# A hand-ordered attention and feed-forward kernel: a new order of the same words, whole score steps from the start, the residual sum written into its own input tile

## The chip, the cores and the metric

The kernel runs on one core of one Trainium2 chip. The core has a matrix engine (PE, whose weight loads the profile lists apart as PEld), a vector engine (DVE), an activation engine (ACT), a general engine (POOL) and a queue processor that here only issues DMAs (SP). Each engine works through its own instructions in order; semaphores tie the engines together. The metric is the device time of one launch in microseconds (us); lower is better.

## The reference, cut to what matters

Attention with a hash mask, then layer norm and a two-layer feed-forward with a residual sum. Batch 4, 8 heads, 768 positions, head size 64, model width 512, hidden width 2048.

```python
q_bits = (np.einsum('bhsd,dk->bhsk', q, proj) > 0)        # 6 bits for each query; the same for keys
mask   = q_bucket[:, :, :, None] == k_bucket[:, :, None, :]
scores = np.where(mask, scale * q @ k.T, -1e9)
attn   = softmax(scores)
x      = (attn @ v) brought to [batch, seq, 512]
xn     = (x - mean) / sqrt(var + 1e-6) * g_ln
out    = x + relu(xn @ w_ch1) @ w_ch2
```

## The kernel before

The work is cut into 12 units `u`, three for each batch; a unit has 256 queries of all 8 heads. The heads are two groups `g` of four. A unit and a group have three score steps, each for 256 keys (`kp`), so step `s` runs from 0 to 71 with `u = s // 6`, `g = (s % 6) // 3`, `kp = s % 3`. The mask is not applied as such: for each query and key the six bits, held as +0.5 and -0.5 in the tile `G`, are multiplied with each other by PE and added to the score before the exponential, so that only an equal bucket gives a weight that is not negligible. A row in which no key has the query's bucket must give the mean of the values, so the sum of the values over all 768 positions (`vsB`) is added with a factor of 2 to the power of -100.

Nothing in the program decides the order. The text `ORDER` lists some 1,100 words, `name.engine.numbers`, and a loop at the end calls a function for each word, in that order (engine: `t` PE, `v` DVE, `a` ACT, `p` POOL, `s` SP). Each engine thus gets its instructions in the order of its words; waits come from the tiles that the words read and write, and from their buffers. The words that matter here:

- `lx`, `LX`: load queries or keys (128 to 768 KB) of batch 0 or of a later batch into an `X` tile (4 buffers). `lv`: values (768 KB for batch 0, 192 KB each for later ones) into `vnat` (2 buffers). `lw1`, `lw2`: a quarter of a weight matrix, issued by POOL, since it is cast to bf16 on the way. `lg`: the norm's gain.
- Batch 0: `tn` (DVE) transposes a third of a tile, `ca` casts it (queries, t = 0, with a factor; keys, t = 1), `ha` (PE, fp32, 4 matmuls, line 312) projects onto the hash vectors with the matrix `pfull` that `pf` builds, `bi` (DVE) makes bits. Later batches: `tu` (DVE, eight a head group) transposes into a `T` tile (2 buffers), `CA` casts it, `hm` (PE, line 403) projects, `bt` (DVE) makes bits, and 16 `mo` copies (DMAs of 4.5 KB) bring them to `G`.
- `cv` (POOL) casts values into `vaug`; `on` writes its column of ones. `su` (POOL, lines 369 to 371) adds the values up over 6 blocks; `sp` (PE, line 376) sums over the 128 partitions with a matrix of ones; `sc` copies the result to `vsB`.
- `S.t.s.h` (PE, line 438): the scores of a step, 24 matmuls in sets of four that lie on four strips of 32 rows, into two tiles of two PSUM banks each, `scA` for heads 0 and 1, `scB` for 2 and 3. With h = 2 the word does all four heads, with 0 or 1 only two of them. `E.a.s.h` (ACT, line 444): the exponential of one tile. `A.t.s.h` (PE, line 453): 16 matmuls of the weights with `vaug`, into the tile `acc` (two banks), summed over three steps.
- `na`, `nb`, `nc` (DVE): normalize `acc` into `x(u)` and take statistics. `ce` (DVE, lines 482 and 483): mean, variance, and the centred tile `xc`. `rs` (POOL): 1 / sqrt(var). `fl` (SP): transposes `xc` by DMA into `xnT`; for unit 0 `ft` (PE) and `fc` do this instead.
- `F.t.u.p` (PE, line 510): 8 matmuls, two of the 16 blocks of the hidden layer, into one bank `f1` (unit 0: `f1` and `f2` in turn). `R` (DVE line 520 or ACT line 518): relu into `hb`. `D.t.u.t.q` (PE, line 526): a quarter of the second layer, 4 matmuls of 512 columns into the bank `f2`; the last half tile of unit 11 in 256 columns, with `scA` and `scB`. `Z` (DVE, line 534): the result times 1 / sqrt(var), plus `x`. `O` (line 544): stores 32 partitions of the result.

PSUM is full: scA 2, scB 2, acc 2, f1 1, f2 1 banks. So the next S must wait for E, the next F for R, the next D for Z, the next group's A for na.

In `ORDER` of before, the steps 2, 1 and 0, with which the kernel begins, are done as halves (`S.t.2.0`, `S.t.2.1` and so on); all later ones whole. SP issues nearly all DMAs: ACT issues the load of `proj` and six of the last stores.

Of the kernel before, what the change touches and what calls it, by code (L numbers as in the profile page):

```python
# [8 lines left out]
F32 = mybir.dt.float32  # L9
# [29 lines left out]
F.t.1.1 R.v.1.1 A.t.12.2 A.t.13.2 F.t.1.0 R.v.1.0 S.t.15.2 E.a.15.1 mo.s.1.0.2.1 LX.s.2.0.1 F.t.1.5 R.v.1.5
mo.s.1.0.3.0 lw2.p.3 D.t.0.0.3 mo.s.1.0.3.1 E.a.15.0 mo.s.1.0.1.2 hm.t.1.1 S.t.17.2 E.a.17.0 E.a.17.1 mo.s.1.0.1.3  # L40
su.p.1.4 mo.s.1.0.2.0 na.v.2.0 A.t.16.2 nb.v.2.0 A.t.15.2 nc.v.2.0 bt.v.1.1 mo.s.1.1.1.0 mo.s.1.1.0.0 mo.s.1.1.0.3
mo.s.1.1.2.0 mo.s.1.1.3.1 F.t.1.7 mo.s.1.1.3.2 Z.v.0.0 D.t.0.1.0 S.t.18.2 E.a.18.0 E.a.18.1 CA.v.1.1.0 tu.v.2.0.1.3
tu.v.2.0.1.0 R.v.1.7 A.t.17.2 mo.s.1.1.1.3 mo.s.1.1.1.1 F.t.1.4 R.a.1.4 mo.s.1.1.1.2 D.t.0.1.1 D.t.0.1.2 sp.t.1.0
sc.a.1.0 mo.s.1.1.0.1 na.v.2.1 nb.v.2.1 nc.v.2.1 ce.v.2.0 fl.s.2.0 ce.v.2.1 D.t.0.1.3 mo.s.1.1.0.2 F.t.1.3 R.v.1.3
S.t.20.2 E.a.20.0 E.a.20.1 F.t.1.6 Z.v.0.1 D.t.1.0.0 D.t.1.0.1 D.t.1.0.2 rs.p.2 R.a.1.6 D.t.1.0.3 CA.p.1.1.1
tu.v.2.0.0.2 sp.t.1.4 fl.s.2.1 mo.s.1.1.2.2 tu.v.2.0.1.1 mo.s.1.1.3.3 S.t.19.2 E.a.19.1 mo.s.1.1.2.3 mo.s.1.1.3.0
mo.s.1.1.2.1 tu.v.2.0.0.1 O.s.0.1 sc.v.1.4 F.t.2.7 O.s.0.2 cv.p.1.0.2 lv.s.2.0.0 lv.s.2.0.1 A.t.18.2 A.t.20.2
cv.p.1.4.2 lv.s.3.0.1 rs.p.1 Z.v.1.0 LX.s.2.1.0 R.v.2.7 F.t.2.4 R.v.2.4 E.a.19.0 S.t.21.2 E.a.21.0 D.t.1.1.0
E.a.21.1 O.s.0.0 F.t.2.0 A.t.19.2 lv.s.2.0.3 tu.v.2.0.1.2 na.v.3.0 nb.v.3.0 tu.v.2.0.0.3 R.a.2.0 lv.s.2.0.2 S.t.22.2
E.a.22.0 E.a.22.1 F.t.2.1 R.a.2.1 su.p.2.0 LX.s.2.1.1 A.t.21.2 D.t.1.1.1 LX.s.3.0.0 tu.v.2.0.0.0 S.t.23.2 E.a.23.1  # L50
# [12 lines left out]
ce.v.4.1 fl.s.4.1 rs.p.4 D.t.3.0.1 S.t.35.2 E.a.35.0 E.a.35.1 hm.t.2.1 bt.v.2.1 mo.s.2.1.2.1 tu.v.3.0.0.2
mo.s.2.1.0.2 tu.v.3.0.1.1 tu.v.3.0.0.1 mo.s.2.1.0.3 mo.s.2.1.2.2 mo.s.2.1.1.0 D.t.3.0.2 F.t.3.6 R.a.3.6 O.s.2.2
mo.s.2.0.2.2 mo.s.2.1.3.1 lv.s.2.4.0 cv.p.2.4.0 mo.s.2.1.0.1 mo.s.2.1.3.2 mo.s.2.1.2.3 S.t.34.2 E.a.34.1 E.a.34.0
# [52 lines left out]
def kernel(  # L118
# [15 lines left out]
    nc = tc.nc  # L134
# [78 lines left out]
    def xt(u):  # L213
        return sb(f"x{u}", [P, 2, DM], F32, "x", 3)
# [374 lines left out]
```

## Time and profile before

| what | us |
|---|---|
| median of 3 runs | 313.65 |
| lowest and highest run | 312.13, 322.8 |
| span of the profiled execution | 311.1 |

The span runs from the first to the last instruction of the profiled execution; the time of a run also has what lies around it, about 2.5 us. The busy time of PE contains waiting inside a run of matmuls, since a matmul's end is modelled. More of the profile's rows:

| group (line, engine) | instructions | mean ns | busy us |
|---|---|---|---|
| f, first layer (510, PE) | 768 | 273 | 99.3 |
| sc, scores (438, PE) | 1728 | 267 to 273 | 96.0 |
| acc, weights times values (453, PE) | 1152 | 194 | 44.6 |
| exponential (444, ACT) | 144 | 1110 | 152.7 |
| relu (520, DVE) | 52 | 690 | 35.9 |
| relu (518, ACT) | 44 | 597 | 26.1 |
| transpose of a later batch (243, DVE) | 48 | 553 | 24.9 |
| query cast of a later batch (252, POOL) | 3 | 4243 | 12.7 |
| sums of values (369, 370, 371, POOL) | 24 | 1819, 853, 809 | 27.9 |
| copy to G (415, issued by SP) | 96 | 721 | |

Eight instructions of 273 ns that start 109 ns apart take 0.87 us, not 8 x 273: on PE the distance of starts counts. The profile's chain of waits goes back from the last instruction to what released it, step by step; "issue" in it is time in which an engine waited for nothing that the profile shows. DMAs moved 33.58 MB, most of it in the first 54 us. The granted clock of PE was 0.998 over the span.

### The profile page before, as it was taken

How to read it: one execution, taken by the hardware profiler on the slowest of the kernel's cores; microseconds unless marked ns; L12 is line 12 of the kernel's file. 1: busy time of each engine (PE TensorE's matmuls, PEld its weight loads, DVE VectorE, ACT ScalarE, POOL GpSimd, SP SyncE). 2: the span in 40 equal slices, each digit the busy share in tenths (PEclk: the TensorE clock that was granted, in tenths of full speed). 3: DMA queues.
4: the chain of work that ended last, by engine and by line, in shares of the span. 5: the costliest groups of instructions: out<-in, count | busy, mean ns of one | idle time of the engine just before them, and what ended most of it. 6: DMA issues, size and time to landing. Idle time of an engine off the chain costs nothing.

```text
span 311.1 us, 9787 instructions
## 1 busy us (share of the span) xinstructions
PE 294.3 (95%) x4296; PEld 206.5 (66%) x4336; DVE 185.7 (60%) x357; ACT 181.5 (58%) x197; POOL 89.7 (29%) x103
## 2 busy tenths in 40 slices
PE   7997799799999899989999999999999999999995
PEld 6675587576677557667667666667667676775663
DVE  3578868768442984978364668443544547246432
ACT  2666687454678655665456787655666777661000
POOL 0869570602403650416705304300300101001000
PEclk9999999999999999999999999999999999999999
DMA  7999999840299317511430901401300400502122
GB/s 177 286 301 361 238 208 261 91 125 9 42 244 300 128 24 179 166 38 35 100 79 2 204 8 30 87 11 33 94 2 2 103 0 13 93 2 60 43 70 68
DMA packets 30426, 33.58 MB, mean 108 GB/s; under 512 B 15536, under 2 KB 27056, under 8 KB 30384
## 3 DMA queue, kind: packets, MB, share of 16 engines
q1 hardware_dynamic: 25792, 28.50, 36.0%
q0 software_dynamic: 4224, 4.19, 8.3%
q8 instruction: 34, 0.56, 0.7%
q10 hardware_dynamic: 368, 0.26, 0.3%
q14 instruction: 8, 0.07, 0.1%
HBM read 27.53 MB, written 6.29 MB: 109 GB/s over the span
## 4 chain that ended last, share of the span: by engine, by line
PE 73%; DMA 14%; POOL 4%; DVE 4%; issue 3%; SPq 1%; DVEq 0%; POOLq 0%
PE f L510 25%; PE sc L438 13%; PE acc L453 8%; DMA vn<-in_v_dram 8%; DMA w_sb<-in_moe_w_ch_dram 5%; POOL t L369 2%; PE hp L403 1%; POOL vaug L361 1%; DMA xnT<-xc 1%; PE f_100None L526 1%; PE f L526 1%; PE f_81None L526 1%; PE f_50None L526 1%; PE f_60None L526 1%; PE f_90None L526 1%
## 5 line engine op out<-in xcount | busy, mean ns | idle before, releaser
L444 ACT ACTIVATE E<-sc,bias_sb 128x1024 bf16<-128x1024 f32 x144 | 152.7, 1110 | 72.3 <-PE sc L438 71.3
L510 PE MATMUL f<-xnT,w_sb 128*128 128x256 bf16 x768 | 99.3, 273 | 1.5 <-DVE B L246 1.2
L510 PEld LDWEIGHTS <-w_sb 128*128 128x128 bf16 x768 | 70.9, 98 | 23.6 <-issue 10.0
L520 DVE TENSOR_SCALAR hb<-f 128x512 bf16<-128x512 f32 x52 | 35.9, 690 | 58.9 <-PE f L510 58.3
L526 PEld LDWEIGHTS <-hb 128*128 128x128 bf16 x400 | 37.5, 98 | 36.0 <-issue 5.1
L438 PE MATMUL sc<-qb,kb 32*128 32x256 bf16 x1152 | 53.4, 267 | 0.0
L518 ACT ACTIVATE hb<-f 128x512 bf16<-128x512 f32 x44 | 26.1, 597 | 39.5 <-PE f L510 39.5
L453 PEld LDWEIGHTS <-E 128*128 128x128 bf16 x1152 | 41.1, 98 | 6.5 <-issue 4.3
L438 PE MATMUL sc<-G 6*128 6x256 bf16 x576 | 42.6, 273 | 2.4 <-DVE G L246 1.3
L453 PE MATMUL acc<-vaug,E 128*128 128x65 bf16 x1152 | 44.6, 194 | 0.0
L488 POOL TENSOR_SCALAR rs<-mv 128x2 f32<-128x2 f32 x12 | 7.1, 594 | 99.8 <-DVE mv L482 99.5
L438 PEld LDWEIGHTS <-kb 32*128 32x128 bf16 x1152 | 31.1, 93 | 1.6
L438 PEld LDWEIGHTS <-G 6*128 6x128 bf16 x576 | 15.6, 91 | 22.2 <-issue 18.2
L243 DVE STREAM_TRANSPOSE T<-X 128x384 f32<-128x384 f32 x48 | 24.9, 553 | 0.8 <-POOL kb L254 0.8
L369 POOL TENSOR_TENSOR t<-vn 128x768 f32<-128x768 f32 x8 | 14.6, 1819 | 33.4 <-DMA vn<-in_v_dram 33.3
L466 DVE SCALAR_TENSOR_TENSOR y<-vsB,acc 128x520 f32<-128x520 f32 x24 | 16.6, 691 | 10.9 <-PE acc L453 10.8
L483 DVE SCALAR_TENSOR_TENSOR xc<-x,mv,gB 128x512 bf16<-128x512 f32 x24 | 22.5, 938 | 0.8
L252 POOL TENSOR_SCALAR qb<-T 128x1536 bf16<-128x1536 f32 x3 | 12.7, 4243 | 28.4 <-DVE mv L482 15.5
L361 POOL CAST vaug<-vn 128x768 bf16<-128x768 f32 x16 | 13.5, 854 | 20.1 <-DMA vn<-in_v_dram 20.1
L475 DVE TENSOR_TENSOR x<-y,rc 128x512 f32<-128x512 f32 x24 | 18.7, 778 | 0.8
L479 DVE BATCH_NORM_STATS2 st<-x 128x6 f32<-128x256 f32 x48 | 18.0, 417 | 0.7
L312 PE MATMUL hf<-tp,pfull 128*128 128x256 f32 x48 | 14.9, 450 | 0.7 <-DVE pfull L277 0.7
(96 smaller groups left out, 229.6 us busy)
## 6 DMA issues: line engine op xcount, KB each, us to landing
out_dram<-res SPq DMA_DIRECT2D x44, 128.0 KB
X<-in_k_dram SPq DMA_DIRECT2D x7, 768.0 KB
vn<-in_v_dram SPq DMA_DIRECT2D x24, 192.0 KB
X<-in_q_dram SPq DMA_DIRECT2D x6, 768.0 KB
w_sb<-in_moe_w_ch_dram POOLq DMA_DIRECT2D x8, 512.0 KB, 12.5
vn<-in_v_dram SPq DMA_DIRECT2D x2, 768.0 KB
G<-B SPq DMA_DIRECT2D x96, 4.5 KB
X<-in_q_dram SPq DMA_DIRECT2D x2, 512.0 KB
```

Of the source, the lines that this page charges most:

```text
L243: nc.vector.transpose(d[:, j], s[:, j, kj0 : kj0 + n])
L369: nc.gpsimd.tensor_tensor(t3, s[:, 0:3], s[:, 3:6], op=AOP.add)
L438: nc.tensor.matmul(sc(s, i // 2)[:, i % 2, 256 * kk : 256 * kk + 256], lh, rh, start=(rep == 0), stop=(rep == 2), skip_group_check=True,)
L444: nc.scalar.activation(E(s)[:, heads(h)], sc(s, h), AF.Exp, scale=EXP_SCALE, bias=bias_sb)
L453: nc.tensor.matmul(acc[:, qt, (D + 1) * i : (D + 1) * (i + 1)], E(s)[:, i, 256 * kk + P * qt : 256 * kk + P * qt + P], vaug(u // 3)[:, 4 * ...
L475: nc.vector.tensor_tensor(xo, a[:, :, :, 0:D], rc.to_broadcast([P, 2, 4, D]), op=AOP.mult)
L479: nc.vector.bn_stats(stats(u)[:, qt, g], xt(u)[:, qt, 256 * g : 256 * g + 256])
L483: nc.vector.scalar_tensor_tensor(xc(u)[:, t], xt(u)[:, t], mv(u)[:, t, 0:1], gB, op0=AOP.subtract, op1=AOP.mult,)
L510: nc.tensor.matmul(f1[:, n].rearrange("p (t x) -> p t x", t=2), w1_sb[:, dt, P * nt : P * nt + P], xnT(u)[:, :, dt], start=(dt == 0), stop ...
L518: nc.scalar.activation(hb(u)[:, 2 * p : 2 * p + 2], f1, AF.Relu)
L520: eng.tensor_scalar_max(hb(u)[:, 2 * p : 2 * p + 2], f1, 0.0)
L526: nc.tensor.matmul(f2, hb(u)[:, nt, P * t : P * t + P], w2_sb[:, nt, half(h)], start=(nt == 0), stop=(nt == NNT - 1),)
```

## The change

Four edits and a new `ORDER`.

- A score tile's banks: for the steps 2, 1, 0 (`ROT`) the six half-step tiles go in turn over scA, scB and acc. In `ORDER` these three steps are now whole words (`S.t.2.2`, `A.t.2.2`).
- `Z` writes its result into `x(u)`, `O` stores from there, and the tile `res` (2 buffers) is gone. `x` and `E` have 4 buffers in place of 3. So a buffer of `x` comes free when its stores have landed.
- For batch 0 the two `su` and `sp` words are replaced by `sq`: six matmuls of ones with `vaug` itself, summed in PSUM.
- The order is new everywhere, and so are some engines: 27 `mo`, 7 `lv`, 3 `LX`, one `lx` and 27 `O` words (6 before) are issued by ACT; the query casts of later batches on POOL are one (`CA.p.2.0.0`) in place of three; `R` stands 55 times on DVE (52 before); all `sc` are on DVE.

```diff
+ROT = (2, 1, 0)
...
     def xt(u):
-        return sb(f"x{u}", [P, 2, DM], F32, "x", 3)
+        return sb(f"x{u}", [P, 2, DM], F32, "x", 4)
...
-    def res(u):
-        return sb(f"res{u}", [P, 2, DM], F32, "res", 2)
...
     def E(s):
-        return sb(f"E{s}", [P, 4, 512], BF16, "E", 3)
+        return sb(f"E{s}", [P, 4, 512], BF16, "E", 4)
...
+    def sq(eng, b, hs):
+        p = ps(f"vp{b}{hs}", [P, 512], "f1")[:, :256].rearrange("p (h d) -> p h d", d=D)
+        for kj in range(KJ):
+            nc.tensor.matmul(p, ones, vaug(b)[:, hs : hs + 4, kj, 0:D], start=(kj == 0), stop=(kj == KJ - 1))
...
     def sc(s, h):
-        return ps(f"sc{s}{h}", [P, 2, 512], ("scA", "scB")[h])
+        tag = ("scA", "scB", "acc")[(2 * ROT.index(s) + h) % 3] if s in ROT else ("scA", "scB")[h]
+        return ps(f"sc{s}{h}", [P, 2, 512], tag)
...
     def Z_(eng, u, t, h=None):
         nc.vector.scalar_tensor_tensor(
-            res(u)[:, t, half(h)], made[f"f2_{u}{t}{h}"], rstd(u)[:, t : t + 1], xt(u)[:, t, half(h)],
+            xt(u)[:, t, half(h)], made[f"f2_{u}{t}{h}"], rstd(u)[:, t : t + 1], xt(u)[:, t, half(h)],
...
-            out=out_view[u // 3][u % 3][c][:, t, half(h)], in_=res(u)[32 * c : 32 * c + 32, t, half(h)],
+            out=out_view[u // 3][u % 3][c][:, t, half(h)], in_=xt(u)[32 * c : 32 * c + 32, t, half(h)],
```

The new order from its beginning to the first F words:

```text
mem.v pmem.p warm.t lx.s.0.0.0.1 lx.s.0.1.1.3 lp.a pf.v tn.v.0.0.0 ha.t.0.0.0 tn.v.0.1.2 lx.s.1.0.0.1 tab.a
bi.v.0.0.0 ca.a.0.0.0 tn.v.0.1.1 lx.s.0.1.0.1 ha.t.0.1.2 bi.v.0.1.2 ha.t.0.1.1 ca.a.0.1.2 S.t.2.2 tn.v.0.1.0
lx.a.0.0.1.3 tn.v.1.0.0 E.a.2.0 bi.v.0.1.1 lx.s.1.1.0.3 ha.t.1.0.0 ca.v.1.0.0 bi.v.1.0.0 ca.p.0.1.1 p32.p lv.s.0.0.4
ca.p.0.1.0 S.t.1.2 tn.v.1.1.0 ha.t.0.1.0 bi.v.0.1.0 tn.v.1.1.1 ca.p.1.1.0 E.a.2.1 ca.p.1.1.1 E.a.1.0 S.t.0.2
cv.p.0.0.0 on.p.0 lv.s.0.4.4 cv.p.0.0.2 ha.t.1.1.1 bi.v.1.1.1 tn.v.1.1.2 lg.s ca.p.1.1.2 cv.p.0.4.0 ha.t.1.1.0
bi.v.1.1.0 E.a.1.1 E.a.0.0 cv.p.0.4.2 lx.s.1.0.1.3 E.a.0.1 LX.s.1.0.1 S.t.4.2 E.a.4.0 lw1.p.3 tn.v.0.0.1 E.a.4.1
ha.t.1.1.2 A.t.2.2 lv.s.1.4.2 A.t.1.2 S.t.3.2 lv.s.1.4.0 bi.v.1.1.2 tn.v.1.0.2 lv.s.1.4.3 sq.t.0.0 E.a.3.0
tu.v.1.0.1.0 LX.s.1.1.0 ca.p.0.0.1 lw1.p.2 A.t.0.2 sc.v.0.0 E.a.3.1 lv.s.1.0.2 tn.v.1.0.1 ca.a.1.0.1 ha.t.0.0.1
tu.v.1.0.1.2 na.v.0.0 S.t.5.2 E.a.5.0 E.a.5.1 lv.s.1.0.0 A.t.3.2 bi.v.0.0.1 sq.t.0.4 sc.v.0.4 S.t.8.2 E.a.8.0
nb.v.0.0 nc.v.0.0 E.a.8.1 tu.v.1.0.1.1 lw1.p.1 A.t.4.2 lv.s.1.4.1 A.t.5.2 ha.t.1.0.1 tn.v.0.0.2 ca.a.0.0.2 bi.v.1.0.1
S.t.6.2 cv.p.1.4.0 E.a.6.0 na.v.0.1 E.a.6.1 ha.t.1.0.2 lw1.p.0 lw2.p.1 nb.v.0.1 nc.v.0.1 bi.v.1.0.2 ha.t.0.0.2
S.t.7.2 A.t.8.2 ce.v.0.1 lw2.p.0 LX.s.1.0.0 bi.v.0.0.2 E.a.7.0 ce.v.0.0 ft.t.0.1 fc.v.0.1 A.t.6.2 ft.t.0.0
tu.v.1.0.0.2 ca.v.1.0.2 E.a.7.1 fc.a.0.0 tu.v.1.0.0.1 LX.a.1.1.1 S.t.9.2 lw2.p.2 tu.v.1.0.0.3 E.a.9.1 A.t.7.2
tu.v.1.0.1.3 E.a.9.0 F.t.0.6 rs.p.0 R.v.0.6 na.v.1.0 F.t.0.7 R.a.0.7 su.p.1.4 S.t.10.2 sp.t.1.4 sc.v.1.4 F.t.0.5
...
```

Two stretches further on, and the end:

```text
...
tu.v.1.1.1.3 mo.s.1.0.1.0 mo.a.1.0.3.0 R.v.1.0 na.v.2.0 F.t.1.2 R.a.1.2 S.t.15.2 E.a.15.1 nb.v.2.0 Z.v.0.0
tu.v.1.1.1.0 mo.s.1.0.0.3 hm.t.1.1 bt.v.1.1 mo.s.1.1.3.1 su.p.1.0 mo.s.1.1.1.1 D.t.0.1.0 F.t.1.1 mo.s.1.1.0.2
...
na.v.3.1 E.a.24.1 hm.t.2.0 bt.v.2.0 CA.p.2.0.0 mo.s.2.0.0.1 LX.a.2.1.1 mo.s.2.0.2.2 S.t.26.2 F.t.2.3 E.a.26.0
nb.v.3.1 A.t.24.2 R.v.2.3 mo.s.2.0.2.1 E.a.26.1 D.t.1.1.3 LX.s.2.1.0 mo.s.2.0.3.2 F.t.2.2 nc.v.3.1 O.s.0.0 ce.v.3.0
...
O.a.10.1 O.a.10.0 O.a.9.0 D.t.11.0.2 R.a.11.7 D.t.11.0.3 O.a.9.1 D.t.11.1.2.0 O.a.8.1 Z.v.11.0 D.t.11.1.3.0
O.a.11.0.3 O.a.11.0.0 O.s.10.3 O.s.11.0.1 D.t.11.1.1.1 D.t.11.1.2.1 Z.v.11.1.0 O.a.11.1.2.0 O.s.11.0.2 O.s.11.1.0.0
O.a.11.1.3.0 O.s.11.1.1.0 D.t.11.1.3.1 Z.v.11.1.1 O.s.11.1.3.1 O.a.11.1.2.1 O.s.11.1.0.1 O.a.11.1.1.1
```

In the order before, the words that the prediction names stand so: `tn.v.0.0.0 pf.v`; `su.p.0.4 sp.t.0.4` between `A.t.4.2` and `S.t.8.2`; `lw1.p.3` after `E.a.2.1`; `su.p.1.0 cv.p.1.0.0` on POOL ahead of `lw2.p.2` and `lw2.p.1`; `CA.p.2.0.0`, `CA.p.2.1.0` and `CA.p.3.0.0` on POOL.

## The prediction

> **What bounds the kernel now.** I read the page first: engine totals, slices, chain.
>
> ```profile
> span 311.1 us, 9787 instructions
> ...
> PE 294.3 (95%) x4296; PEld 206.5 (66%) x4336; DVE 185.7 (60%) x357; ACT 181.5 (58%) x197; POOL 89.7 (29%) x103
> ...
> DMA  7999999840299317511430901401300400502122
> ...
> PE 73%; DMA 14%; POOL 4%; DVE 4%; issue 3%; SPq 1%; DVEq 0%; POOLq 0%
> ```
>
> PE fills 95% of the span, and the DMA share stands at 8 or 9 tenths only in the first seven slices (to about 54 us). The chain in order of time says where which of the two ends last:
>
> ```profile
> 24.89 1.78 POOL t L369
> 26.74 0.81 POOL t L370
> 27.82 9.25 DMA vn<-in_v_dram
> ...
> 42.32 14.57 DMA w_sb<-in_moe_w_ch_dram
> ...
> 153.61 0.87 PE f L510 x8
> 154.48 0.78 PE sc L438 x24
> ...
> 163.79 0.97 PE acc L453 x32
> ...
> 175.81 1.44 PE hp L403 x32
> ...
> 289.44 0.86 PE f_100None L526 x4
> ```
>
> To 57 us it runs through value loads, POOL's value sums and weight loads, afterwards almost only through PE. These rows also price a word: F 0.87, S 0.77, A (16 matmuls) 0.49, a D quarter 0.86, hm 1.44. An ha has four matmuls, at most 1.13 (row of 14.17 us). PE's work is 96 x 0.87 + 96 x 0.86 + 72 x 0.77 + 72 x 0.49 + 6 x 1.44 + 12 x 1.13 = 279, and entering an S costs 0.1 more (last f matmul at 150.73, first sc at 150.94, where two f are 0.11 apart): 286. PE works from 5.44 to 307.0, 301.6, so some 16 us are waits; no order can win more. The table of waits names the large ones:
>
> ```profile
> PE f_00None L526 <- DMA w_sb<-in_moe_w_ch_dram: 1.6, 1, 1.6
> ...
> PE f L510 <- DVE B L246: 1.2, 1, 1.2
> ...
> PE vp L376 <- DVE B L246: 1.0, 1, 1.0
> PE vp L376 <- POOL vsum L371: 0.9, 1, 0.9
> ```
>
> Weighed by the Trainium skill, "Perfetto Trace Analysis", section "Identifying the Most-Contended Engine": matmul busy time is a poor measure of the room left, the busy share of weight loads a better one. By it 34% of 311.1 = 106 us would be open; the matmul starts 0.11 apart say that the room is 16, and I go by them.
>
> **The change, part by part.** All sums are against the profiled execution: span 311.1, median 313.65, so 2.55 lie around it.
>
> *Head, to the first F word.* Before: F.0.7 at 39.01. Work ahead of it: 12 ha 13.6, ten S (three as halves) 8.7, eight A 3.9, small words 0.6 = 26.8 in the 33.6 since 5.44; 6.8 us of waits. After, followed by hand along the queues with the row durations: pfull precedes the first transposes, but k lands at 6.68 as before, so the start wins nothing. S.2 goes at about 9.8 (10.36 before). The steps 2, 1, 0 as whole words over scA, scB and acc let S.1 and S.0 start without their predecessor's E, but S.1 waits for the bits of key pair 1, and the six E of 1.11 end at 17.9 against 18.23: 0.3. POOL loses the two sums of batch 0 (1.81 + 0.80 + 0.72 and alike) and PE gains 12 matmuls of 0.11, 1.3, in two sq words less two sp: +1.1. sq needs only vaug, cast by about 21.4; before, sp.0.4 held S.8.2 till 28.59. After, S.8.2 stands at 26.5 (na.0.0, behind a transpose that waits for a key load, holds A.3.2 for 0.5). DVE's chain na, nb, nc, bi, ce (0.70, 0.93, 0.75, 0.42, 0.98) then leads to ft.0.0 at 35.8 and F.0.6 at 37.5, with A.6 already done (0.49): -2.0. DVE rows beside the removed POOL sums show 1.16 where 0.43 is usual (25.79 us), so another 0.5: **-2.5**. Bounds: -4.5 (the waits fall to 2.3) and +1.5 (key or value loads land 2 to 4 us later than at the pace of before, as lx and LX now come ahead of them).
>
> *Weights.* lw2.1 was issued at 42.3 behind a sum that waited for values (37.33), and D.0.0.1 waited 1.65 in it. After, no wait for a sum lies ahead of lw2.1, 2.0, 2.2; only cv.1.4.0 does, so they go at about 30 to 33. In return lw1.3 moves from 8.8 to 22. Landings 2.5 apart (39.5, 42.1, 44.6, 47.1) put w1.0 near 44 and w2.2 near 53; PE wants them at 46 and 56. **-1.65**, bounds -1.65 and +4.
>
> *T tiles of batch 1.* They come free when hm.1.0 ends; eight transposes of 0.55, CA 0.95, R 0.69 and Z 0.75 stand on DVE ahead of hm.1.1: **+0.3**, bounds 0 and 1.5.
>
> *Middle.* The 1.2 us wait has this cause:
>
> ```profile
> 128.74 4.08 POOL L252 TENSOR_SCALAR qb<-T 128x1536 bf16<-128x1536 f32 x1 [15.48 <-DVE mv L482]
> 128.78 3.71 DVE L483 SCALAR_TENSOR_TENSOR xc<-x,mv,gB 128x512 bf16<-128x512 f32 x1
> ...
> 133.01 1.03 PE L510 MATMUL f<-xnT,w_sb 128*128 128x256 bf16 x8 [1.21 <-DVE B L246]
> ```
>
> The xc step takes 0.75 elsewhere; beside POOL's 4 us query cast it ended only with the cast. bt waited behind it, f1 behind bt. After, one such cast stays on POOL (CA.p.2.0.0) where three stood, and CA.v.2.1.0 costs DVE 0.95. In the same way bt.2.0 no longer stands behind ce. -1.2 - 1.0, and -0.2 for the xnT wait at 227: **-2.4**, bounds -2.4 and 0. The remaining cast can meet nb.3.1 with R.v.2.3 behind it: **+0.4**, bounds 0 and 3.
>
> *DMAs moved to ACT.* 27 G copies of 0.72 (SP's row, none on ACT shown), 21 more outputs of 0.40 and 11 loads of 0.43: 33 us more of ACT, which was free for 130. On SP they cost nothing, since it waits 56.7 and 52.4 us for DVE. On ACT an issue delays the E or R behind it. In 16 of the S words an ACT DMA stands between S and its second E; E needs 2.12 and the next S mostly comes 2.2 or more later, so up to 0.4 is lost where the cover is tight: 16 x 0.4 = 6.4 at most, below zero not, since nothing of ACT is shortened. The built program also makes each SP or ACT DMA wait until the one eight places earlier has landed; nearly all of these lie 4 us of PE work or more back. I take **+0.4**, near the lower end, as 49 of the 65 stand outside such a pair. The skill, "DMA: Bandwidth & Descriptors", "Issuing engines are not separate DMA queues", says that issuing from several engines saves sequencer time only; by it the move gains at most what SP had on the path, here nothing, and the sum is the same.
>
> *x tile and buffers.* Without res, x and E have four buffers. nb.4.0, nb.5.0 and nb.11.0 now wait for an output issued at the same place in the order (0.40 for the issue; the trace's last outputs land 1.3 to 1.7 after it); the R words behind them have 3 to 5 us of PE work as cover: **+0.1**, bounds 0 and 2; with the cover gone each costs 1 to 2. One A more in flight for E: 0.
>
> *Tail.* The last output on ACT waits for the landing of one issued under 2 us before: **+0.4**, bounds 0 and 0.9.
>
> Sum: -2.5 - 1.65 + 0.3 - 2.4 + 0.4 + 0.4 + 0.1 + 0.4 = -4.95; span 306.15, time **308.7**.
>
> **Rivals.** *A, no waits left*: head -4.5, the weights -1.65, and of PE's idle between 60 and 300 us (240 - 234.83 = 5.2) two thirds go, 3.5: 304.0. For it: every wait named above has a cause that the new order touches; against: DVE's chain in the head stays. *B, weights late*: the first weight is issued 13 us later, and the median landing is 12.5. If w1.0 and w2.2 come 4 us late, 308.7 + 4 = 312.7. *C, slower*: ACT is held. If the G copies cost ACT their whole 0.72 ahead of an E and no cover helps, 16 x 0.72 = 11.5: 320.2. For it: SP shows trains of eleven such copies, 8.7 us long, and an ACT DMA whose slot is held by one of them waits too; then E, S and PE. It decides once ACT loses more than some 2 us per unit in stages where S follows S within 2.2. Against: ACT has 40% free. That the three whole steps do not overlap would change 0.3.
>
> **How the numbers follow.** Forecast 0.50 with its own range 305.5 to 312, from the bounds of head and middle; A 0.22; B 0.10; C 0.18. About 2% (6.3 us, 307.4 and 319.9) is what a measurement can tell here. Of the forecast 0.18 lies below 307.4 and 0.32 within: faster 0.18 + 0.22 = 0.40, same 0.32 + 0.10 = 0.42, slower 0.18. The range leaves out C and the best of A: 303 to 317.
>
> **What would show it.** The first f matmul at about 37.5 instead of 39.0; no wait of S.8.2 for vsum; no DMA wait in D.0.0; DVE's xc under 1 us near the end of unit 4; PE's idle in 60 to 300 us near 3. Wrong if the first f comes after 39, if PE waits for w_sb in a unit 0 F word, or if E's idle time names DMA or issue and sc waits for E.

## The result, and the profile after

| | before | after |
|---|---|---|
| median, us | 313.86 (312.13 to 322.8, 4 runs) | 316.96 (316.58 to 318.38, 4 runs) |
| ratio, with its 95% interval | | 1.0133 (1.0084 to 1.0183) |
| span of the profiled execution, us | 311.1 | 314.8 |

The change made the kernel 1.3% slower, where 308.7 was forecast. The ratios, here and below, leave out executions clearly longer than the others of the same kernel (322.8 us is one; the profiled ones of e5_head, e8_all and h4_again are others, so that nothing below rests on their spans). The page of the changed kernel shows engine totals, PE's row and its clock in 40 slices of 7.9 us, DMA, and the shares of the chain that ended last:

```profile
span 314.8 us, 9790 instructions
PE 293.9 (93%) x4301; PEld 206.4 (66%) x4346; DVE 180.8 (57%) x362; ACT 180.2 (57%) x192; POOL 76.3 (24%) x97
...
PE   8986999978979999999999999999999999999993
...
PEclk9997999999999999999999999999999999999998
DMA  7999999571651671246371200420310111303034
...
PE 65%; DMA 16%; SPq 7%; POOL 5%; ACT 2%; issue 2%; DVE 1%; ACTq 0%; POOLq 0%; DVEq 0%
```

PE's busy time is that of before; 93% in place of 95% means that PE stood still longer. In the chain PE has fallen from 73% to 65%, and SP's queue, 1% before, has 7%. A slice of the clock shows 7 tenths, where before no slice did. The table of busy times by stretch (columns: stretch and its length, then busy time of PE, PEld, DVE, ACT and POOL with the number of instructions, granted clock, DMA share, GB/s) tells where. The rows of before come first, then those of after:

```profile
60.00:300.00 240.00, 234.83 (x3467) 162.13 (x3494) 141.30 (x254) 142.92 (x156) 56.25 (x57) 1.00 0.32 75
60.00:100.00 40.00, 39.49 (x626) 27.54 (x622) 23.35 (x44) 24.86 (x28) 9.25 (x11) 1.00 0.54 137
```

```profile
60.00:300.00 240.00, 230.60 (x3394) 159.41 (x3436) 136.77 (x258) 138.94 (x148) 50.49 (x58) 1.00 0.30 75
60.00:100.00 40.00, 34.95 (x514) 23.61 (x521) 20.77 (x40) 21.90 (x25) 13.03 (x17) 1.00 0.43 110
```

PE's idle time between 60 and 300 us is 9.4, where the prediction had said near 3, and 5.05 of it lies between 60 and 100 us, where before had 0.51. The table of waits of the changed kernel (who waited, for whom; sum, times, longest) names what PE and ACT waited for:

```profile
ACT E L447 <- DMA G<-B: 6.3, 3, 2.4
...
PE acc L456 <- DVE y L469: 3.7, 1, 3.7
PEld L441 <- DMA G<-B: 3.6, 3, 1.9
...
ACT hb L521 <- DMA G<-B: 2.7, 1, 2.7
...
PE sc L441 <- DMA G<-B: 2.7, 2, 1.6
...
PE hp L405 <- ACT hb L521: 1.6, 1, 1.6
```

Of the rows in which PE waited before, the weights and the two for B are gone, as forecast, and POOL's sum is down from 0.9 to 0.3. New are the copies to `G`, which had cost 0.4 in all, a DVE step that holds A, and an R that holds hm. As to DMA as a whole, the text ahead of the prediction has most of the 33.58 MB moved in the first 54 us; the DMA view of the kernel before, cut to the first 54.4 us, gives 14.24 MB, that is 42%.

**The copies.** The chain of waits between 60 and 92 us, its DMA steps and what they release (start, length, what):

```profile
61.27 7.09 DMA vn<-in_v_dram
...
76.69 1.82 DMA G<-B
78.51 0.05 issue
78.56 0.83 PE sc L441 x22
...
86.24 5.39 DMA G<-B
91.63 0.05 issue
91.67 0.50 PE sc L441 x9
```

A copy of 4.5 KB takes 1.82 us from its issue when little is under way; the one of 86.24 took 5.39, and S.22.2 stands 2.46 us in it. Two value chunks had been issued ahead of it, one by ACT at 85.48 and one by SP at 85.74, and a key load of 768 KB, issued at 84.45, landed only at 89.08. The Trainium skill, "DMA: Bandwidth & Descriptors", section "Queues, rings and completion order", says that on each DMA engine descriptors are consumed in ring order. That agrees with the landings here: the chunk that SP had issued ahead landed at 91.41, the copy behind it at 91.63.

S.20.2 stands 1.36 us for another reason. Its copy, the one of 76.69, landed in the ordinary 1.82 us; it was issued late. Eight copies of hash group 1.1, which PE needed later, stand ahead of it in SP's order, and SP itself had stood still. SP's own row among the waits:

```profile
SPq L417 <- DMA vn<-in_v_dram: 3.8, 1, 3.8
```

From 64.6 to 68.4 us SP waited for a completion slot that a value load held (61.27 in the chain above, landed 7.09 us later), and from 69.2 to 70.0 for another. Of the 3.8 us not all is the load's, since the bits of group 1.1, which SP was to copy next, were ready only at 66.7. In the kernel before all 16 copies of group 1.0 stand ahead of those of group 1.1, and PE waited for none, though a 768 KB load stands among them there too.

**The hold on ACT.** The timeline around 63 us (start, length, engine, line, operation; in brackets the idle time and what ended it):

```profile
61.23 1.04 PE L513 MATMUL f<-xnT,w_sb 128*128 128x256 bf16 x8
...
63.12 0.79 ACTq L417 DMA_DIRECT2D G<-B  x1
63.96 0.60 ACT L521 ACTIVATE hb<-f 128x512 bf16<-128x512 f32 x1 [2.70 <-DMA G<-B]
64.45 2.11 ACT L447 ACTIVATE E<-sc,bias_sb 128x1024 bf16<-128x1024 f32 x2
64.61 1.51 PE L405 MATMUL hp<-T,p 128*32 128x192 f32 x32 [1.57 <-ACT hb L521]
```

F.1.2, the first row, was done at 62.27. Ahead of its R on ACT stands `mo.a.1.0.3.0`, which waits for its completion slot, that is for the landing (63.10) of the copy eight DMAs earlier, issued at 60.51. R goes 1.7 us late, and hm.1.1 with it.

**The head.** The timeline around 25 us:

```profile
23.62 0.58 DVE L240 STREAM_TRANSPOSE T<-X 128x384 f32<-128x384 f32 x1 [2.69 <-DMA X<-in_k_dram]
...
25.56 0.66 DVE L469 SCALAR_TENSOR_TENSOR y<-vsB,acc 128x520 f32<-128x520 f32 x1
...
26.28 0.95 PE L456 MATMUL acc<-vaug,E 128*128 128x65 bf16 x14 [3.75 <-DVE y L469]
```

S.5.2 started at 21.65, 2.9 us earlier than before. Then `tu.v.1.0.1.0`, a transpose for the next batch, waited on DVE for keys that landed at 23.59, and `na.v.0.0` stood behind it. PE stood still for 3.75 us (3.85 by the count used below), and right after that its clock was halved (the same columns as above; 0.50 is the granted clock):

```profile
22.30:26.20 3.90, 0.23 (x9) 0.00 (x0) 2.58 (x7) 0.99 (x2) 0.69 (x1) 0.98 1.06 260
26.20:29.40 3.20, 3.12 (x42) 2.24 (x46) 1.06 (x5) 1.65 (x2) 0.00 (x0) 0.50 1.23 250
```

**The balance.** For each pair of neighbouring PE words, the distance of their starts (of each word's first weight load) beyond what such a pair takes undisturbed (its 15th percentile over all runs) is counted as a wait; a halved clock counts too. The rest is PE's work. The percentile puts the sum of the waits far above the 16 us of the prediction, so only differences between runs say something, and those to some 0.5 us. The forecast's +0.4 for DMAs on ACT stands whole in 60 to 100, though the prediction spread it over the kernel. All in us, of the profiled executions:

| stretch | 0-60 | 60-100 | 100-300 | 300 on | waits | work | last matmul to end |
|---|---|---|---|---|---|---|---|
| before | 12.7 | 2.8 | 19.0 | 0.3 | 34.8 | 270.7 | 4.2 |
| after | 11.1 | 8.1 | 17.3 | 0.9 | 37.4 | 270.8 | 5.2 |
| forecast of the difference | -4.15 | +0.7 | -1.9 | +0.4 with the end | | | |
| difference | -1.6 | +5.3 | -1.7 | +0.6 | +2.6 | +0.1 | +1.0 |

### The profile page after: what moved, and what is told of

Its sections match the earlier page's. It is cut to its first block, busy times and chain, and to the rows that moved or that the text cites. A ratio compares the mean times of both kernels' runs of the same rounds, so it can differ in the third digit from the quotient of the medians.

```text
span 314.8 us, 9790 instructions
## 1 busy us (share of the span) xinstructions
PE 293.9 (93%) x4301; PEld 206.4 (66%) x4346; DVE 180.8 (57%) x362; ACT 180.2 (57%) x192; POOL 76.3 (24%) x97
## 4 chain that ended last, share of the span: by engine, by line
PE 65%; DMA 16%; SPq 7%; POOL 5%; ACT 2%; issue 2%; DVE 1%; ACTq 0%; POOLq 0%; DVEq 0%
PE f L513 22%; PE sc L441 12%; DMA vn<-in_v_dram 9%; PE acc L456 8%; DMA X<-in_q_dram 4%; SPq L417 4%; DMA G<-B 3%; PE hp L405 2%; ACT E L447 2%; POOL t L366 2%; PE f_100None L529 1%; PE f L529 1%; PE f_81None L529 1%; PE f_60None L529 1%; PE f_41None L529 1%
## 5 line engine op out<-in xcount | busy, mean ns | idle before, releaser
L523 DVE TENSOR_SCALAR hb<-f 128x512 bf16<-128x512 f32 x55 | 38.0, 690 | 58.2 <-PE f L513 57.4
L441 PE MATMUL sc<-G 6*128 6x256 bf16 x576 | 44.6, 274 | 5.0 <-DMA G<-B 2.7
L456 PE MATMUL acc<-vaug,E 128*128 128x65 bf16 x1152 | 45.5, 194 | 3.7 <-DVE y L469 3.7
L521 ACT ACTIVATE hb<-f 128x512 bf16<-128x512 f32 x41 | 24.4, 597 | 39.8 <-PE f L513 31.2
L441 PEld LDWEIGHTS <-G 6*128 6x128 bf16 x576 | 16.8, 91 | 25.4 <-issue 18.6
L358 POOL CAST vaug<-vn 128x768 bf16<-128x768 f32 x16 | 14.4, 910 | 42.8 <-DMA vn<-in_v_dram 33.5
L478 DVE TENSOR_TENSOR x<-y,rc 128x512 f32<-128x512 f32 x24 | 17.9, 748 | 3.7 <-DMA out_dram<-x 2.9
L486 DVE SCALAR_TENSOR_TENSOR xc<-x,mv,gB 128x512 bf16<-128x512 f32 x24 | 19.3, 803 | 0.9
L482 DVE BATCH_NORM_STATS2 st<-x 128x6 f32<-128x256 f32 x48 | 17.8, 415 | 0.4
L366 POOL TENSOR_TENSOR t<-vn 128x768 f32<-128x768 f32 x6 | 11.1, 1851 | 19.8 <-DMA vn<-in_v_dram 19.8
L251 POOL CAST kb<-T 128x1536 bf16<-128x1536 f32 x5 | 7.8, 1556 | 31.2 <-DVE T L240 31.2
L309 PE MATMUL hf<-tp,pfull 128*128 128x256 f32 x48 | 13.3, 412 | 0.3 <-DVE tp L240 0.3
```

The lines of the kernel that those rows point to most:

```text
L366: nc.gpsimd.tensor_tensor(t3, s[:, 0:3], s[:, 3:6], op=AOP.add)
L441: nc.tensor.matmul(sc(s, i // 2)[:, i % 2, 256 * kk : 256 * kk + 256], lh, rh, start=(rep == 0), stop=(rep == 2), skip_group_check=True,)
L456: nc.tensor.matmul(acc[:, qt, (D + 1) * i : (D + 1) * (i + 1)], E(s)[:, i, 256 * kk + P * qt : 256 * kk + P * qt + P], vaug(u // 3)[:, 4 * ...
L478: nc.vector.tensor_tensor(xo, a[:, :, :, 0:D], rc.to_broadcast([P, 2, 4, D]), op=AOP.mult)
L482: nc.vector.bn_stats(stats(u)[:, qt, g], xt(u)[:, qt, 256 * g : 256 * g + 256])
L486: nc.vector.scalar_tensor_tensor(xc(u)[:, t], xt(u)[:, t], mv(u)[:, t, 0:1], gB, op0=AOP.subtract, op1=AOP.mult,)
```

## The experiments

Ratios are to the kernel before, measured on the same chip beside each group of runs. Words in a diff are words of `ORDER`; what is not shown stays. The stretch columns are those of the balance, each from one execution. The changed kernel's own ratio came out as 1.0133 and 1.0196 on two occasions, so differences of 0.6% or less between runs of different groups are not told apart.

| run | ratio (95%) | span | 0-60 | 60-100 | 100-300 |
|---|---|---|---|---|---|
| changed kernel | 1.0133 (1.0084 to 1.0183) | 314.8 | 11.1 | 8.1 | 17.3 |
| the same, second time (e9_after) | 1.0196 (1.0078 to 1.0314) | 315.7 | 10.0 | 9.3 | 17.9 |
| e1_tu | 1.0223 (1.0136 to 1.0311) | 316.9 | 11.6 | 7.8 | 18.9 |
| e2_hold | 1.0264 (1.0223 to 1.0304) | 318.8 | 11.4 | 7.7 | 20.8 |
| e3_loads | 1.0152 (1.0063 to 1.0242) | 317.9 | 16.8 | 4.8 | 17.8 |
| e4_three | 1.0225 (1.0078 to 1.0373) | 316.3 | 13.7 | 4.0 | 20.4 |
| e5_head | 1.0018 (0.9969 to 1.0067) | 314.5 | 11.1 | 6.5 | 18.5 |
| u1_su | 1.0275 (1.0238 to 1.0312) | 319.1 | 13.2 | 8.3 | 18.0 |
| u2_rot | 1.0238 (1.0208 to 1.0268) | 317.4 | 9.5 | 10.9 | 18.2 |
| u3_sp | 1.0469 (1.0415 to 1.0522) | 327.9 | 11.6 | 10.9 | 25.3 |
| e6_copies | 1.0117 (1.0025 to 1.0208) | 315.0 | 12.4 | 4.8 | 18.9 |
| e7_both | 1.003 (0.9986 to 1.0075) | 312.0 | 9.7 | 5.4 | 18.5 |
| e8_all | 1.0005 (0.996 to 1.005) | 314.4 | 11.3 | 6.3 | 18.9 |
| h1 | 0.9984 (0.9928 to 1.004) | 311.3 | 11.9 | 4.6 | 17.5 |
| h2 | 0.9881 (0.9772 to 0.999) | 306.7 | 9.3 | 2.6 | 17.8 |
| h2_again | 0.9889 (0.98 to 0.9977) | 308.8 | 11.5 | 2.7 | 17.4 |
| h3 | 1.0426 (1.0251 to 1.0601) | 324.4 | 20.4 | 5.5 | 18.5 |
| h4_again | 0.9962 (0.9903 to 1.0021) | | | | |

### Three repairs inside the new order, and all three

```diff
 # e1_tu
- tu.v.1.0.1.0 ... tu.v.1.0.1.2 na.v.0.0 ... nb.v.0.0 nc.v.0.0
+ na.v.0.0 ... nb.v.0.0 nc.v.0.0 tu.v.1.0.1.0 tu.v.1.0.1.2
```

> The changed kernel with two words moved on DVE: the transposes tu.v.1.0.1.0 and tu.v.1.0.1.2 of the next batch's keys stand behind nc.v.0.0 instead of ahead of sc.v.0.0 and na.v.0.0. Theory (the new order gives its head gain back because DVE waits 2.69 us for that key load, which lands at 23.59, and PE then sits 3.85 us before A.3.2 and its granted clock halves for 3.4 us): A.3.2 goes from 26.3 to about 22.5, the halved clock goes, F.0.6 from 39.3 to about 35.5; span 314.8 - 4 to -5 = 310 to 311. Rival (the loads of the head are the limit, whatever stands on DVE): the next value or key load holds PE instead, F.0.6 stays above 38, span within 1.5 of 314.8.

A.3.2 went to 22.59 and F.0.6 to 35.37, as expected, and hm.1.0 came at 51.98, 0.7 later than in the changed kernel. In the timeline PE met the next wait at F.0.5, behind `sp.1.4`:

```profile
40.88 0.72 POOL L368 TENSOR_TENSOR vsum<-t 128x256 bf16<-128x256 f32 x1
41.65 0.27 PE L373 MATMUL vp<-vsum,ones 128*128 128x256 bf16 x1 [3.58 <-POOL vsum L368]
```

This sum of the next batch (`su.p.1.4`) ended at 41.6 here and at 42.3 in the changed kernel; the weights for F.0.2 landed at 41.95. The halved clock moved to 42.7. So the key load was one wait in front of another, and its removal won nothing, as the rival had said.

```diff
 # e2_hold
- mo.a.1.0.3.0 R.v.1.0 na.v.2.0 F.t.1.2 R.a.1.2 S.t.15.2 E.a.15.1
+ R.v.1.0 na.v.2.0 F.t.1.2 R.a.1.2 S.t.15.2 E.a.15.1 mo.a.1.0.3.0
 # mo.a.2.0.0.0 O.a.0.2 behind E.a.31.1; mo.a.2.1.0.2 behind E.a.33.1
```

> The changed kernel with four DMAs of ACT moved behind the ACT work that they stood in front of: mo.a.1.0.3.0 behind E.a.15.1 (was ahead of R.a.1.2), mo.a.2.0.0.0 and O.a.0.2 behind E.a.31.1, mo.a.2.1.0.2 behind E.a.33.1 (was ahead of R.a.4.4 and E.a.33.0). Theory (ACT is held while such a DMA waits for its slot; PE lost 1.64 before hm.1.1, 0.65 in S.27.2, 1.04 in S.37.2): these three go, span -3.3 = 311.5. Rival (PE waits there for something else that comes as late, T tiles or copies to G): less than 0.7 us won.

hm.1.1 came 1.4 us earlier, and S.20.2 then waited 3.05 for its copy in place of 1.36. At 142 us the moved copy showed the hold in its pure form, for it now stood ahead of R.a.4.0 with no slot free for 3.5 us:

```profile
145.23 0.75 ACTq L417 DMA_DIRECT2D G<-B  x1
146.03 0.60 ACT L521 ACTIVATE hb<-f 128x512 bf16<-128x512 f32 x1 [4.34 <-DMA G<-B]
...
146.68 1.03 PE L513 MATMUL f<-xnT,w_sb 128*128 128x256 bf16 x8 [2.58 <-ACT hb L521]
```

The hold is real, but where it stood in the changed kernel a wait for copies stood right behind it.

```diff
 # e3_loads
- lv.s.1.0.3 ... lv.s.1.0.1 ... LX.s.2.0.0 ... LX.a.2.0.1 ... mo.s.1.1.3.1 ... mo.s.1.0.2.0 ... mo.s.1.0.3.2
+ lv.s.1.0.3 lv.s.1.0.1 LX.s.2.0.0 LX.s.2.0.1 fl.s.1.1 ... mo.s.1.0.2.0 mo.s.1.0.3.2 mo.s.1.1.3.1
```

> The changed kernel with the loads lv.s.1.0.3, lv.s.1.0.1, LX.s.2.0.0 and LX.2.0.1 (from ACT to SP) issued ahead of fl.s.1.1, and the copies mo.s.1.0.2.0 and mo.s.1.0.3.2 ahead of the first of hash group 1.1. Theory (S.20.2 and S.22.2 wait 1.36 and 2.46 us for copies to G, since the SP queue stood 3.8 and 0.9 us behind these loads' slots and took copies of the wrong group first): both waits under 0.5, span -3 to -3.8 = 311 to 312. Rival (SP's own issue time of 0.75 us a copy is the limit from 52 to 88 us): at most 1 us won, S.22.2 still waits for G.

Both waits for copies went (60 to 100 us: 8.1 to 4.8), as the theory said. The edit also puts `mo.s.1.0.2.0` and `mo.s.1.0.3.2` ahead of the copies of group 1.1, so for S.20.2 it doesn't tell the loads from the order of the copies. Loading earlier had its price: SP had been idle, issued the loads at once at 25 to 44 us, and the weights w1.1 landed at 47.0 in place of 39.9: F.0.2 waited 3.7 and the clock was halved for 6.8 us. e4_three, all three together, had the gain of the first in the head, lost it to the same weights (w1.1 at 44.6), and waited 2.4 and 1.5 at 142 us as e2_hold did.

> The changed kernel with the three edits together (two transposes later on DVE, four ACT DMAs behind their E or R, four loads and two copies earlier on SP). Theory (three separate waits): the gains add up to about 11 us, span about 304, time about 306.5, faster than the kernel before by 2%. Rival (one wait is hidden by another, or weights and values bind once the head is 4 us earlier): half of it, span 309.

Each of the three removed the wait that it was aimed at, and none saved time.

### The head with its loads and sums in another order; parts of the change undone

```diff
 # e5_head: e1_tu, and
- LX.s.1.1.0 lv.s.1.4.2 lv.s.1.4.0 lv.s.1.4.3 lv.s.1.4.1 ... LX.s.1.0.0
+ LX.s.1.0.0 LX.s.1.1.0 lv.s.1.4.2 lv.s.1.4.0 lv.s.1.4.3 lv.s.1.4.1
 # su.p.1.4 sp.t.1.4 sc.v.1.4 to about 80 us; cv.p.1.4.0 behind lw2.p.3; F.0.4 ahead of F.0.2
```

> The changed kernel with its head alone rearranged: the two key transposes later on DVE (as in the first experiment, which lost its 3.9 us again at F.0.5 to the sum su.p.1.4 on POOL and at F.0.2 to the weights w1.1), su.p.1.4 with sp and sc later, LX.s.1.1.0 and the four value loads lv.1.4 behind LX.s.1.0.0, cv.p.1.4.0 and lw2.p.3 behind CA.p.1.0.1, F.0.4 ahead of F.0.2. Theory (the head's loss is in the order of its loads and sums, a wait behind each wait): F.0.6 at about 35.4, no wait over 0.5 at F.0.5 and the next, hm.1.0 at about 47.5 instead of 51.3, span -3.5 = 311. Rival (until 52 us the number of bytes sets the pace, whatever their order): hm.1.0 stays above 50.5, span within 1 of the changed kernel's 314.8.

hm.1.0 came at 47.74, as expected, and the kernel drew level with before: 1.0018. The gain met a larger wait at hm.1.1 (2.9 us, the same copy on ACT) and another halved stretch.

```diff
 # u1_su
- sq.t.0.0 ... sq.t.0.4
+ su.p.0.0 ... sp.t.0.0 ... su.p.0.4 ... sp.t.0.4
 # u2_rot
-ROT = (2, 1, 0)
+ROT = ()
 # u3_sp: 27 mo, 7 lv, 3 LX, 1 lx
- mo.a.  lv.a.  LX.a.  lx.a.
+ mo.s.  lv.s.  LX.s.  lx.s.
```

> The changed kernel with the value sums of batch 0 undone: su and sp (POOL adds, one matmul of ones) in place of sq, su.p.0.0 behind ca.p.1.1.2 and su.p.0.4 behind cv.p.0.4.2 on POOL. Theory (sq was a gain and the loss lies in the order): POOL's 3.4 us a sum push lw1.p.3 and all weights some 7 us later and sp waits; span +2 to +4. Rival (the 12 matmuls of ones are what the change lost): span -1 or better.

Slower again by what was expected, though not by the path expected: the weights landed no 7 us later (the first at 34.2 against 32.9, w1.0 at 42.4 against 44.6); PE waited 3.2 at A.4.2 and 1.2 at S.8.2, and the clock was halved from 28.3 on for 6.8 us. In this order, sq is a gain (1.0275 without it, 1.0133 and 1.0196 with it).

> The changed kernel with ROT empty: the first three whole steps use scA and scB only. Theory (the head ends with a key load at 23.6, so what comes before it has 3 us to spare): S.1.2 and S.0.2 up to 1.5 later, A.3.2 still at about 26.3, span within 0.5 of 314.8. Rival (the rotating banks set the head): span +1 or more, or, if acc held them up, -0.5.

A miss for the theory. Score step 1 waits for the exponential of step 2, 1.2 us by the balance's count and 0.72 on its row:

```profile
12.17 0.28 PE L441 MATMUL sc<-G 6*128 6x256 bf16 x2 [0.72 <-ACT E L447]
```

The head made that good (hm.1.0 at 49.37), but 60 to 100 us took 10.9 in waits and two halved stretches. That the banks alone cost nothing is in h4_again below; why this order fell out worse without them is not settled, and 1.0238 lies only 0.4% above the second of the changed kernel's own ratios.

> The changed kernel with all loads and copies to G that ACT issues (27 mo, 7 lv, 3 LX, 1 lx) issued by SP at the same places; only the outputs stay on ACT. Theory (ACT's issues cost about 3.3 us of holds, but SP's queue is the limit from 52 to 88 us, where it gets some 11 more issues): the holds go and S.20.2 and S.22.2 wait longer for copies to G; span 315 to 319. Rival (the issues on ACT are the whole loss): span -3 or better.

1.0469. The theory's direction, far beyond its size, and against rival C: with this order, ACT's issues are a relief for SP. Waits for `G` doubled (the wait table of this run, to be held against 3.6 and 2.7):

```profile
PEld L441 <- DMA G<-B: 7.2, 5, 2.0
PE sc L441 <- DMA G<-B: 6.3, 4, 1.8
```

F words waited too, 5.3 us in three waits for `xnT`, which SP also issues, and the clock was halved in five stretches.

### No load among the copies; both; small moves; the changed kernel again

```diff
 # e6_copies
- lv.s.1.0.3 ... lv.s.1.0.1 ... mo.a.1.0.3.0 ... (ten loads of batch 2 and 3 between copies)
+ lv.s.1.0.3 lv.s.1.0.1 (behind lv.s.1.4.1) ... mo.s.1.0.3.0 ...
+ mo.s.1.1.3.2 LX.s.2.0.0 LX.s.2.0.1 lv.s.2.0.2 lv.s.2.0.1 lv.s.2.4.1 lv.s.2.0.3 LX.s.3.0.1 lv.s.2.0.0 lv.s.2.4.2 lv.s.2.4.0
 # tu.v.2.0.* behind these loads; e7_both: with e5_head
 # e8_all: e7_both with mo.a.2.0.0.0 O.a.0.2 mo.2.1.0.2 fl.s.5.0 fl.s.7.1 R.v.2.2 ca.a.1.0.1 moved
```

> The changed kernel with only the traffic between 50 and 90 us rearranged: no load is issued among the copies to G. The value chunks lv.1.0.3 and lv.1.0.1 go early (behind lv.s.1.4.1), the ten loads of batch 2 and LX.3.0.1 behind the last copy of hash group 1.1 and all on SP, the transposes of batch 2 and su.p.2.0 behind them, the copies mo.1.0.2.0 and mo.1.0.3.2 ahead of hash group 1.1, mo.1.0.3.0 on SP instead of ACT. Theory (a 4.5 KB copy that is issued behind a 768 KB load lands with it, 7 us instead of 1.8 us later, and holds slots of eight meanwhile, which holds SP, ACT and PE): the waits before hm.1.1 (1.64), in S.20.2 (1.36) and in S.22.2 (2.46) fall to under 0.5 each; span -4 to -5 = 310 to 311. Rival (SP's own 0.75 us for each of 32 copies sets that pace): at most 1.5 won.

In 60 to 100 us 8.1 became 4.8, and no score matmul waits for `G` any more; but copies of group 1.0 were moved ahead here as well. 1.6 of it came back after 100 us: around hm.2.0, which now waits 1.4 for the transposes that were moved, and ahead of D.2.0.0, where F.2.5 waits 1.46 on its row for an R on DVE. The ratio, 1.0117, can't be told from the changed kernel's, nor the span, 315.0 from 314.8: by time, the rival was right.

> The changed kernel with the rearranged head of the experiment before last (hm.1.0 3.5 us earlier) and the rearranged traffic of the run before together. Theory (two separate losses of the new order): -3.5 and -4.5 add up, span 306 to 307, time about 308.5, ratio to the kernel before 0.98. Rival (with an earlier head the copies, which SP sends one by one, come later than PE all the same): span 310.

1.003, between a third (by the span) and 40% (by the ratio) of the gain that was expected. It can't be told from e5_head's 1.0018: with the better head, taking the traffic away too brought nothing that the ratio shows.

> The run before with seven small moves more: mo.a.2.0.0.0 and O.a.0.2 behind E.a.31.1, mo.2.1.0.2 on SP, fl.s.5.0 and fl.s.7.1 right behind their ce, R.v.2.2 ahead of ce.v.3.0, ca.a.1.0.1 behind E.a.5.1. Theory (the smaller waits of S.27.2 1.2, S.37.2 0.3 to 1.0, F.5.3 1.5, F.7.3 0.8, D.2.0.0 0.7, A.4.2 1.0 have these causes): span -3 to -4 against the run before, about 303. Rival (each is covered by another wait): within 1 of it.

No change against e7_both, as the rival had said. One of the small moves set POOL's query cast beside DVE's xc step at 105.3 to 109.4, 4.12 and 3.46 us, the collision that the prediction described for the kernel before.

> The changed kernel itself once more, beside the three above on the same chip: span 314.8 and ratio 1.013 within 0.5% if its waits are the same in each execution.

The ratio is 1.0196. In this execution the key load landed at 22.09, A.3.2 lost 1.2 instead of 3.9 and hm.1.0 came at 48.97, 2.3 earlier; the span is not shorter. That the ratio would repeat within 0.5% and the waits with it did not come. The chain of this execution has the same two copies:

```profile
75.59 1.83 DMA G<-B
84.90 5.20 DMA G<-B
```

What the head wins, the copies take: 0 to 60 us 11.1 and 10.0, 60 to 100 us 8.1 and 9.3.

### The two orders spliced at 50 us

```diff
 # h1: changed code; changed order up to R.a.0.1, then
+ on.p.1 su.p.1.0 cv.p.1.0.0 CA.p.1.0.1 F.t.0.3 R.a.0.3 and the order of before from fl.s.1.0 on
 #     (LX.s.2.0.0 lv.s.1.0.3 lv.s.1.0.1 already behind tu.v.1.0.1.3)
 # h2: h1 with the head of e5_head      h4: the order of before, whole, in the changed code
 # h3: the order of before up to ce.v.1.0, then the changed order
```

> The changed kernel with its own order up to R.a.0.1 (about 49 us, so sq, the whole first steps and the new head stay) and the order of before from there on; LX.2.0.0, lv.1.0.3 and lv.1.0.1 on SP behind the other early loads, and the few words that only the old order had done by then (CA.1.0.1, F.0.3, cv.1.0.0, su.1.0, on.1) at the seam. Theory (the new head is a gain of 2 to 3 us, the new order loses it between 50 and 120 us, where loads stand among the copies to G and DMAs stand on ACT): PE waits in 60 to 120 us fall from about 10 to 5; span 307 to 309, ratio to the kernel before 0.985 to 0.995. Rival (the head's gain meets the same copies in either order, or the loss is spread): ratio 1.00 or more.

0.9984. In 60 to 100 us 4.6, of which 2.0 is one DVE hold at the seam. The waits side with the theory; the time lies near the rival's 1.00.

> As the run before, with the rearranged head (transposes of the next keys and the sum su.1.4 later, four value loads and LX.1.1.0 behind LX.1.0.0) in place of the changed kernel's own. Theory: hm.1.0 another 1 to 3 us earlier, span 306 to 308, ratio 0.98 to 0.99. Rival: within 1 of the run before, since weights and copies are what PE meets.

308.92 us, ratio 0.9881: the fastest kernel of this study and faster than both. Its profile, the page's first row and clock, and PE between 60 and 100 us:

```profile
span 306.7 us, 9797 instructions
...
PEclk9999999999999999999999999999999999999999
```

```profile
60.00:100.00 40.00, 39.45 (x606) 26.91 (x615) 23.54 (x45) 24.74 (x28) 10.91 (x12) 1.00 0.52 158
```

PE is as busy there as before, with hm.1.0 1.5 us earlier, and no stretch of halved clock before the end.

> The spliced kernel with the rearranged head once more, with more rounds, since its first interval reached from 0.977 to 0.999. Theory: 0.985 to 0.99, the profile again without a stretch of halved clock before the end. Rival (that was a quiet quarter of an hour of the chip): 1.00.

0.9889 (0.98 to 0.9977): the ratio holds. That no stretch would have a halved clock did not: this execution has one of 3.41 us, from 7.7 to 11.1 us.

> The other way round: the order of before (halves, su and sp) up to ce.v.1.0 (about 52 us), the changed kernel's order from there on, in the changed code. Theory: the old head, the new loss; hm.1.0 at about 52, waits of about 10 us in 60 to 120; span 316 to 318, ratio 1.015 or more. Rival (the loss comes from the new head alone): span 311 to 312, ratio 1.00.

No evidence: at the seam `sp.1.4` waited 6.8 us for a sum that POOL had been given too late, and the clock was halved for 10.2 us. So the converse of h2 was not measured.

> The order of before, word for word, in the changed code: the result added in the x tile, x and E with 4 buffers, and the banks of the first half steps in turn over scA, scB and acc. Theory (none of these edits costs anything by itself): span 311, ratio 1.00 within 0.5%. Rival (outputs that hold x, or acc used for scores, cost by themselves): ratio 1.01 or more.

This kernel was run once here (311.88 us), too little for a ratio.

> The order of before in the changed code once more; its first measurement gave no verdict, three of four runs were disturbed. Theory (tile and bank edits cost nothing by themselves): ratio 1.00 within 0.5%, span 311. Rival (they cost by themselves): 1.01 or more.

0.9962 (0.9903 to 1.0021): the edits of tiles and banks cost nothing by themselves.

## Why the prediction was wrong

It had the sign wrong. By stretches, its -4.95 and the measured +3.7 of the span part as follows.

- **Where it failed most: 60 to 100 us, +0.7 forecast, +5.3 measured.** The step is "DMAs moved to ACT" with its sentence on SP, "On SP they cost nothing", and "nearly all of these lie 4 us of PE work or more back". I priced each issue, and neither what a copy waits for once it is issued nor what stands ahead of it in SP's queue. The reading that DMA is busy only in the first seven slices was wrong besides: the row shown there has 9 tenths again in slices 12 and 13, from 86 to 101 us. The new order puts five loads among the copies of hash group 1.0 at 57 to 62 us and seven among those of group 1.1 at 72 to 87, and it puts copies of group 1.1 ahead of the last of group 1.0. The two copies that PE needed came 1.36 and 2.46 late, and SP itself stood 3.8 and 0.9 us, most of it for slots that loads held. e3_loads and e6_copies took loads away and moved copies too, and both waits went. Rival C had another part of the mechanism, a DMA on ACT that waits for a slot: 1.64 at hm.1.1, 0.65 at S.27.2 and 1.04 at S.37.2, 3.3 in all, against +0.4 forecast, 0 to 6.4 allowed and 11.5 for the rival. It was not the whole: u3_sp, with none but outputs left on ACT, is 3% slower still.
- **The head and the weights, -4.15 forecast, -1.6 measured.** The weights were right: no wait in D.0.0. In the head the words "behind a transpose that waits for a key load" were priced at 0.5 and cost 3.85 in one execution, 1.2 in the other, plus the halved clock, which had no term. The first F came at 39.32 instead of 37.5, past the "after 39" that the prediction had named as a sign of being wrong. What was wrong in kind is that the sum took a gain in the head for a gain of the kernel: e1_tu and e9_after won 3.9 and 2.7 at F.0.6 and ended no earlier, since the sum on POOL, the weights, and then the copies were next. The prediction's own question, what is late next, was asked at each wait that goes, and not for the stretch behind.
- **100 to 300 us, -1.9 forecast, -1.7 measured.** Right, and by its steps: both xc steps of unit 4 take 0.75 where one had taken 3.71, the waits of 1.55 at 131 and 1.18 at 106 are gone. The +0.4 allowed for the cast that remained was not what came: the query cast (99.25 to 103.36 us) met no xc step, but POOL's key cast (105.36, 1.46 us) ran beside one, which took 1.93, and some 0.7 was lost in front of D.2.0.0 (0.52 on the row).
- **The end, +0.4 forecast, +1.6 measured.** From the last matmul to the end 5.2 us instead of 4.2, and 0.6 more in PE's last words.
- **The x tile and buffers, the rotating banks, sq.** +0.1 for the first was right in size: nb.4.0 waited 2.9 us for an output and no row of PE's names it, and h4_again shows the edits free. sq was a gain in this order, as said (u1_su). "That the three whole steps do not overlap would change 0.3" fits h4_again, and u2_rot speaks against it with a loss of up to 1% whose path stays open.

Of the signs that the prediction named, three came: S.8.2 has no wait for vsum, D.0.0 none for a DMA, xc is under 1 us. Three spoke against it: the first F after 39, PE's idle time of 9.4, and E's idle time that names DMA (6.3 for `G`). That 316.96 lies inside 303 to 317 is luck: the forecast's own bound was 312, B gives 312.7 and C 320.2, and 317 was worked out nowhere. "Same", at 0.42, came with a mechanism that none of the four cases had in full.

What the runs place is the stretch. With the old order from 50 us on, the ratio is 0.9984 (h1), and 0.9881 with the better head as well (h2), which has 2.6 in place of 8.1 in 60 to 100 us; that is some 1.4 to 2% below the kernels that keep the new order there with the same head (1.0133 and 1.0196; 1.0018 for e5_head). The better head is worth some 1% or more with either order behind it. Which difference of the order behind 50 us does it stays open: the loads, the order of the copies and the place of the DMAs on ACT were never changed apart with a gain in time, and the repair of one wait mostly ended at the next.

## What to carry to other kernels

A small transfer that PE needs soon should not be issued behind a large one that nobody needs soon, nor behind small ones that are needed later: cost the order of DMAs by when they land, and count what stands ahead of each in its queue. A wait that is removed is worth what the next one in the same chain leaves of it, so a head gains only as far as the first shared resource behind it (here the copies) gets earlier too. Where two orders are each better in a different stretch, splice them: here that showed which stretch held the loss, and made the fastest kernel.

## What the runs showed of the hardware

PE's granted clock fell to 0.5 for 3.41 us, or two or three times that, in 28 stretches ahead of the end, in 17 of the 20 profiled executions (before, e7_both and the first of h2 had none). In the 3.41 us ahead of each such stretch PE was busy for 0 to 1.98 us. Cut into windows of 3.41 us in step with these stretches, no window with PE busy for less than 1.40 us was without a halved clock behind it; between 1.40 and 1.98 both occur. So waits of some 1.5 us can be enough (e9_after, at 90 us), and 2.46 us (after, at 89 us) can pass. The wait of 3.85 us so cost some 1.6 us more (an estimate: 3.12 us of PE's busy time at half the clock); the 24 matmuls of S.8.2 started over 0.99 us in that stretch, over 0.57 in the kernel before. The Trainium skill, "TensorE: Matmul & The Clock Gate", "Part 1: The HAM clock gate", has the half clock follow an idle window of about 3.4 us; the length agrees, but in all of these windows but one PE was partly busy, and the measurement decides.
